# Group 1's head sum by gather and VectorE adds, and the fourth layernorm's statistics on ScalarE, in a two-layer attention and FFN kernel

## The chip, the cores and the metric

One core of one Trainium2 chip runs the whole program. The metric is the device time of one execution in microseconds (us). In the profile lines PE is TensorE (matmuls), PEld its weight loads, DVE VectorE, ACT ScalarE and POOL GpSimd; the granted clock is the share of TensorE's full clock that was granted. Executions of one kernel here agree within 0.2%; all are in the fast state, except three single runs (e4, e6, e7) whose state is unknown. Much of this document measures inside the trace. For that it uses one stretch, called **the stretch** below: from the start of group 0's head-sum matmuls on PE (the first `L<-big,smat` group, near 64 us) to the first matmul of the QKV stage that follows the output projection of group 1 (near 260 us). PE works in a fixed order, so the two ends are the same instructions in every kernel here. The stretch contains everything that the change touches and leaves out the first 64 us, whose length varies from execution to execution with the first loads.

## The reference

Two layers, each a sliding attention (8 keys per position, at distance 0, 2, ..., 14) and a GELU FFN, both with a layernorm without weights and a residual. Cut to what matters:

```python
# x: 1 x 2048 x 1024; H = 32 heads of 32; W = 8 keys, dilation 2; F = 3584
q, k, v = split(layernorm(x) @ wqkv)
logits  = einsum("bhsd,bhswd->bhsw", q, k[pos - 2*w]) * scale     # head sum over d
attn    = softmax(where(pos - 2*w >= 0, logits, -1e9))            # over the 8 keys
x = x + einsum("bhsw,bhswd->bhsd", attn, v[pos - 2*w]) @ wo
x = x + gelu(layernorm(x) @ w1 + b1) @ w2 + b2
# ... the same two lines once more
```

## The kernel before

The 2048 positions are cut into groups of 512; there are eight (layer, group) pairs, numbered n = 0 to 7. PE does all large products (QKV, output projection "wo", FFN1, FFN2) in one fixed order. The attention between them is VectorE work: `new_prod` multiplies q with the shifted k, a tree of adds leaves one product tile, the *head sum* adds the partitions of one head, `attend` is the softmax, `spread` copies its result to all partitions of the head, and `av` makes one of eight weighted sums of v (written to `oT`, which `wo` reads). Groups 0 and 1 did the head sum on PE, the later groups by a DMA gather and three VectorE adds. A drain is VectorE's reading of a finished PSUM bank, `tmp<-acc`, which releases the bank for PE.

```python
bigp = ctx.enter_context(tc.tile_pool(name="bigp", bufs=3))       # 3 big VectorE tiles
def acc_tile():
    return psum.tile([P, T], F32, name="acc", bufs=6)             # 6 PSUM banks for all products
...
def ln_stats_ahead(g):                       # statistics of a layernorm, ahead of its use
    for tt in range(NTT):
        ln_stats(g * NTT + tt, mv_ahead[:, tt, :], rstd_ahead[:, tt, :])   # 2 bn_stats + bn_aggr on VectorE
...
def head_sum(n, last=True):                  # 8 matmuls, four at a time side by side
    ...
    for wh in range(2):
        for tb in range(NTT):
            mm(L[tb * H:(tb + 1) * H, wh * 4:(wh + 1) * 4, :], lhsT=smat[:],
               rhs=prod[:, tb, wh * 4:(wh + 1) * 4, :], ..., tile_position=(0, tb * H))

def gather(n):                               # the other way: move the 4 partitions of a head side by side
    prod = s["prods"].pop(0)
    Lq = bigp.tile([P, HP, W, P], BF16, name="big")
    for j in range(HP):
        pool.dma_start(Lq[:, j, :, :], prod[j::HP, :, :, :])
...
def attend(n):
    e = smp.tile([P, W, P], F32, name="e")
    if "Lq" in s:                            # after gather: three adds
        vec.tensor_tensor(out=e[:], in0=Lq[:, 0, :, :], in1=Lq[:, 1, :, :], op=ALU.add)
        for j in range(2, HP):
            vec.tensor_tensor(out=e[:], in0=e[:], in1=Lq[:, j, :, :], op=ALU.add)
        L = e
    else:
        head_sum(n)
        L = s.pop("L")
    ...
    if n < 2:
        vec.tensor_reduce(out=mx[:], in_=L[:].rearrange("p w t -> p t w"), axis=AX.X, op=ALU.max)
    else:
        mx = fold(L, ALU.max)
    vec.tensor_tensor(out=e[:], in0=L[:], in1=mx..., op=ALU.subtract)
    act.activation(e[:], e[:], ACT.Exp, scale=SCALE)
    ...
def spread(n):
    if n < 2:                                # through DRAM, because the layout is another
        ...
...
# the order of work; (unit, function) pairs hang VectorE work into PE's stages; hold() keeps VectorE's order
stage(gen_ffn1(0), sides=at(5, attend, 1) + at(5, spread, 1) + at(5, hold) + each(new_prod, 2, 2, 1)
      + at(10, gather, 2) + at(10, hold) + each(av, 1, 10, 2, 0, 4))
stage(gen_ffn2(0), sides=at(0, ln_stats_ahead, 3) + at(15, hold) + at(15, ln_a, 3, None, True)
      + each(av, 1, 16, 1, 4, 8) + at(23, hold))
# then gen_wo(1), which reads oT of group 1, and gen_qkv(3)
```

Of the kernel before, what the change touches and what calls it, by code (L numbers as in the profile page):

```python
# [8 lines left out]
ACT = mybir.ActivationFunctionType  # L9
ALU = mybir.AluOpType  # L10
AX = mybir.AxisListType
BF16 = mybir.dt.bfloat16
F32 = mybir.dt.float32
# [4 lines left out]
def kernel(  # L18
# [18 lines left out]
    P = 128  # L37
    _, S, D = A_x.shape
# [3 lines left out]
    W = 8  # L42
# [3 lines left out]
    EPS = 1e-5  # L46
    SCALE = float(DH) ** -0.5
    T = 512
    NTT = T // P
# [4 lines left out]
    HP = P // H  # L54
# [15 lines left out]
    lnp = ctx.enter_context(tc.tile_pool(name="lnp", bufs=2))  # L70
    xnp = ctx.enter_context(tc.tile_pool(name="xnp", bufs=2))
    attp = ctx.enter_context(tc.tile_pool(name="attp", bufs=1))
    bigp = ctx.enter_context(tc.tile_pool(name="bigp", bufs=3))
# [5 lines left out]
    def acc_tile():  # L79
        return psum.tile([P, T], F32, name="acc", bufs=6)  # L80

    class InOrder:
# [18 lines left out]
        def hold(self):  # L101
            self.floor = self.last

    vec, act, pool, sp = InOrder(nc.vector), InOrder(nc.scalar), InOrder(nc.gpsimd), InOrder(nc.sync)
    last_pe = [None]

    def dep_order(dependent, dependency, why):
        tc.add_manual_dep(dependent.ins, dependency.ins.name,
                          mybir.DependencyInfo(mybir.DependencyClass.NoSync, mybir.DependencyReason.SCHED_ONLY), reason=why)
# [7 lines left out]
    def mm(*args, **kwargs):  # L117
        return pe(nc.tensor.matmul(*args, **kwargs))  # L118

    x = [xpool.tile([P, D], BF16, name=f"x{t}") for t in range(S // P)]  # L120
# [26 lines left out]
    mhalf = const.tile([P, 1], F32, name="mhalf")  # L147
# [14 lines left out]
    mv_ahead = const.tile([P, NTT, 2], F32, name="mv_ahead")  # L162
    rstd_ahead = const.tile([P, NTT, 1], F32, name="rstd_ahead")
# [29 lines left out]
    def ln_stats(t, mv=None, rstd=None):  # L193
        stats = lnp.tile([P, 2, 6], F32, name="stats")
        for h in range(2):
            vec.bn_stats(stats[:, h, :], x[t][:, h * HALF:(h + 1) * HALF])
        if mv is None:
            mv = lnp.tile([P, 2], F32, name="mv")
            rstd = lnp.tile([P, 1], F32, name="rstd")
        vec.bn_aggr(mv[:], stats[:])  # L200
        pool.tensor_tensor(out=rstd[:], in0=mv[:, 1:2], in1=eps_t[:], op=ALU.add)
        pool.tensor_tensor(out=rstd[:], in0=rstd[:], in1=mhalf[:], op=ALU.pow)
        return mv, rstd

    def ln_stats_ahead(g):
        for tt in range(NTT):
            ln_stats(g * NTT + tt, mv_ahead[:, tt, :], rstd_ahead[:, tt, :])

    def ln_norm(t, mv, rstd, xn=None):
        if xn is None:  # L210
# [81 lines left out]
    def head_sum(n, last=True):  # L292

        if "L" not in st[n]:
            st[n]["L"] = psum.tile([P, W, P], F32, name="L", bufs=1)
            start = True
        else:
            start = False
        L = st[n]["L"]
        prod = st[n]["prods"].pop(0)  # L300
# [3 lines that stand above are left out]
                   rhs=prod[:, tb, wh * 4:(wh + 1) * 4, :], start=start,  # L304
                   stop=last, skip_group_check=True, tile_position=(0, tb * H))
# [79 lines left out]
    def gather(n):  # L385

        s = st[n]
        prod = s["prods"].pop(0)
        Lq = bigp.tile([P, HP, W, P], BF16, name="big")
        s["Lq"] = Lq  # L390
        for j in range(HP):
            pool.dma_start(Lq[:, j, :, :], prod[j::HP, :, :, :])

    def fold(e, op):

        t = iop.tile([P, W // 2, P], F32, name="tmp")
        vec.tensor_tensor(out=t[:], in0=e[:, 0:4, :], in1=e[:, 4:8, :], op=op)
        vec.tensor_tensor(out=t[:, 0:2, :], in0=t[:, 0:2, :], in1=t[:, 2:4, :], op=op)
        vec.tensor_tensor(out=t[:, 0, :], in0=t[:, 0, :], in1=t[:, 1, :], op=op)
        return t[:, 0, :]  # L400

    def attend(n):

        s = st[n]
        e = smp.tile([P, W, P], F32, name="e")
        if "Lq" in s:
            Lq = s.pop("Lq")
# [7 lines that stand above are left out]
        if n % NG == 0:  # L415
            p = H if n == 0 else P
            vec.tensor_tensor(out=L[0:p, 0:W - 1, 0:HALO], in0=L[0:p, 0:W - 1, 0:HALO], in1=mask[0:p, :, :], op=ALU.add)
        if n < 2:
            mx = smp.tile([P, P], F32, name="mx")
            vec.tensor_reduce(out=mx[:], in_=L[:].rearrange("p w t -> p t w"), axis=AX.X, op=ALU.max)  # L420
            mx = mx[:]
        else:
            mx = fold(L, ALU.max)
        vec.tensor_tensor(out=e[:], in0=L[:], in1=mx.unsqueeze(1).to_broadcast([P, W, P]), op=ALU.subtract)
        act.on = 1 < n < N - 1
        act.activation(e[:], e[:], ACT.Exp, scale=SCALE)
        act.on = False
        z = smp.tile([P, P], F32, name="z")
        vec.reciprocal(z[:], fold(e, ALU.add))
        a = smp.tile([P, W, P], BF16, name="a")  # L430
        vec.tensor_tensor(out=a[:], in0=e[:], in1=z[:].unsqueeze(1).to_broadcast([P, W, P]), op=ALU.mult)
        s["a"] = a

    def spread(n):

        s = st[n]
        a = s.pop("a")
        abc = attp.tile([P, NTT, W, P], BF16, name="abc")
        s["abc"] = abc
        s["oT"] = attp.tile([P, NCH, T], BF16, name="qT" if n == N - 1 else "oT")  # L440
        if n < 2:
            a_d = dram.tile([H, NTT, W, P], BF16, name="a_d")
            for tb in range(NTT):
                pool.dma_start(a_d[:, tb, :, :], a[tb * H:(tb + 1) * H, :, :])
            a = a_d
        for j in range(HP):
            pool.dma_start(abc[j::HP, :, :, :], a[:])
# [33 lines left out]
    def gen_ffn1(n):  # L481
        xnT = xb.pop(n)
        hT = hpool.tile([P, KF, T], BF16, name="hT")
        st[("h", n)] = hT
        for j4 in range(KF // 4):
            wt = wpool.tile([P, KD, 4 * P], BF16, name="wt")
            load = sp.dma_start(wt[:], w1_v[:, :, j4 * 4 * P:(j4 + 1) * 4 * P])
            if n == 0 and j4 == 1:
                dep_order(load, last_transpose[0], "transposes first")
            for jj in range(4):  # L490
                j = j4 * 4 + jj
                ps = acc_tile()
                for k in range(KD):
                    mm(ps[:], lhsT=wt[:, k, jj * P:(jj + 1) * P], rhs=xnT[:, :, k, :], start=(k == 0), stop=(k == KD - 1))
                act.activation(hT[:, j, :], ps[:], ACT.Gelu_apprx_tanh, bias=b1T[:, j:j + 1])
                yield
# [69 lines left out]
    def stage(gen, count=None, sides=()):  # L566


        u = 0
        while count is None or u < count:  # L570
            if next(gen, gen) is gen:
                break
            for v, f in sides:
                if v == u:
                    f()
            u += 1
        for v, f in sides:
            if v >= u:
                f()

    def at(u, f, *args, **kwargs):
        return [(u, lambda: f(*args, **kwargs))]

    def each(f, n, u0, du, c0=0, c1=NCH):
        return [(int(u0 + du * (c - c0)), lambda c=c: f(n, c)) for c in range(c0, c1)]

    hold = vec.hold
# [5 lines left out]
    with tc.tile_pool(name="early", bufs=1) as early:  # L593
        load_x(1)
        load_x(2)
        stage(gen_qkv(0, qk_next=early), sides=at(14, load_b2))
        q1 = gen_qkv(1, defer=True, qk_pool=early)
        stage(q1, sides=at(6, attend, 0) + at(6, spread, 0) + at(6, hold) + each(new_prod, 1, 8, 1, 0, 4) + each(av, 0, 12, 1))
        q2 = gen_qkv(2, defer=True)
        stage(q2, 18)  # L600
        new_prod(1, 4)
        hold()
        stage(gen_wo(0))
        hold()
        stage(q2, sides=each(new_prod, 1, 0, 1, 5, 8))
    hpool = ctx.enter_context(tc.tile_pool(name="hpool", bufs=1))
    stage(gen_ffn1(0), sides=at(5, attend, 1) + at(5, spread, 1) + at(5, hold) + each(new_prod, 2, 2, 1)
          + at(10, gather, 2) + at(10, hold) + each(av, 1, 10, 2, 0, 4))
    stage(gen_ffn2(0), sides=at(0, ln_stats_ahead, 3) + at(15, hold) + at(15, ln_a, 3, None, True) + each(av, 1, 16, 1, 4, 8) + at(23, hold))
    for n in range(1, N - 2):  # L610
# [10 lines left out]
    n = N - 2  # L621
# [35 lines left out]
```

## Time and profile before

| | before |
|---|---|
| time, first three runs | 1233.37 us (1232.91 to 1234.22) |
| PE busy | 1222.2 of 1230.8 us |
| VectorE busy | 861.9 us (70%) |
| the eight matmuls of group 1's head sum | 0.55 us of PE |
| the stretch | 64.19 to 260.56 = 196.37 us |

The busy line of the page: busy us, share of the span, instructions.

```profile
PE 1222.2 (99%) x5739; PEld 632.6 (51%) x5789; DVE 861.9 (70%) x922; ACT 307.3 (25%) x491; POOL 87.2 (7%) x207
```

PE hardly ever waits. The view of waits on PE lists what waited, for what, the sum, how often, and the longest, in us. All three are in the first 15 us:

```profile
PE acc L219 <- DVE xn L93: 1.5, 1, 1.5
PE acc L118 <- DVE big L93: 1.1, 1, 1.1
PE acc L118 <- DMA wt<-in_A_wqkv_dram: 0.3, 1, 0.3
```

PE's timeline (start, length, operation and shapes, count) shows the head sum of group 1 in the middle of FFN1, then FFN2 (`hT`) and wo(1) (`oT`):

```profile
139.05 20.88 PE L118 MATMUL acc<-xnT,wt 128*128 128x512 bf16 x96
159.86 0.62 PE L118 MATMUL L<-big,smat 128*32 128x512 bf16 x8
160.41 38.16 PE L118 MATMUL acc<-xnT,wt 128*128 128x512 bf16 x176
198.40 48.51 PE L118 MATMUL acc<-wt,hT 128*128 128x512 bf16 x219
246.75 13.54 PE L118 MATMUL acc<-wt,oT 128*128 128x512 bf16 x61
```

The head sum takes the time from 159.86 to 160.41, 0.55 us. VectorE is full in this part of the execution. By stretches (window, its length, then busy us and instructions of PE, PEld, DVE, ACT and POOL, the granted clock, DMA share and GB/s), DVE is busy 37.50 of 39 us and 52.94 of 54 us:

```profile
160.00:199.00 39.00, 38.95 (x186) 17.52 (x180) 37.50 (x22) 18.90 (x26) 4.21 (x8) 1.00 0.52 169
199.00:253.00 54.00, 53.74 (x246) 24.46 (x250) 52.94 (x66) 0.29 (x1) 5.55 (x12) 1.00 0.66 205
```

### The profile page before, as it was taken

How to read it: one execution, taken by the hardware profiler on the slowest of the kernel's cores; microseconds unless marked ns; L12 is line 12 of the kernel's file. 1: busy time of each engine (PE TensorE's matmuls, PEld its weight loads, DVE VectorE, ACT ScalarE, POOL GpSimd, SP SyncE). 2: the span in 40 equal slices, each digit the busy share in tenths (PEclk: the TensorE clock that was granted, in tenths of full speed). 3: DMA queues.
4: the chain of work that ended last, by engine and by line, in shares of the span. 5: the costliest groups of instructions: out<-in, count | busy, mean ns of one | idle time of the engine just before them, and what ended most of it. 6: DMA issues, size and time to landing. Idle time of an engine off the chain costs nothing.

```text
span 1230.8 us, 13962 instructions
## 1 busy us (share of the span) xinstructions
PE 1222.2 (99%) x5739; PEld 632.6 (51%) x5789; DVE 861.9 (70%) x922; ACT 307.3 (25%) x491; POOL 87.2 (7%) x207
## 2 busy tenths in 40 slices
PE   9999999999999999999999999999999999999998
PEld 7666544456444564445544465444654444444444
DVE  7989899988998599375993759937599797011001
ACT  4343152014320143202431024310244101400310
POOL 3010010010010000100011000010000002000000
PEclk9999999999999999999999999999999999999999
DMA  9954665656556654856447565486664558446441
GB/s 290 300 179 143 182 222 185 201 154 209 181 165 215 180 162 163 229 172 186 150 163 238 171 171 170 158 223 202 171 196 145 188 196 208 151 158 196 155 135 52
DMA packets 219391, 225.06 MB, mean 183 GB/s; under 512 B 68194, under 2 KB 187136, under 8 KB 217024
## 3 DMA queue, kind: packets, MB, share of 16 engines
q1 hardware_dynamic: 214704, 208.69, 55.5%
q0 software_dynamic: 4624, 15.49, 3.3%
q8 instruction: 45, 0.74, 0.2%
q14 instruction: 18, 0.15, 0.0%
HBM read 191.11 MB, written 4.72 MB: 159 GB/s over the span
## 4 chain that ended last, share of the span: by engine, by line
PE 99%; DMA 1%; issue 0%; SPq 0%; DVE 0%
PE acc L118 98%; DMA wt<-in_A_wqkv_dram 1%; SPq L93 0%; PE L L118 0%; PE L L219 0%; DVE x L93 0%
## 5 line engine op out<-in xcount | busy, mean ns | idle before, releaser
L118 PE MATMUL acc<-xnT,wt 128*128 128x512 bf16 (+1 forms) x3392 | 720.9, 375 | 0.4 <-DMA wt<-in_A_wqkv_dram 0.3
L118 PEld LDWEIGHTS <-wt 128*128 128x128 bf16 x3392 | 400.5, 119 | 319.1 <-issue 1.4
L118 PE MATMUL acc<-wt,hT 128*128 128x512 bf16 (+1 forms) x1780 | 386.0, 376 | 2.1
L118 PEld LDWEIGHTS <-hT 128*128 128x128 bf16 x1820 | 178.1, 98 | 208.9
L93 DVE TENSOR_TENSOR big<-big 128x1024 bf16<-128x1024 bf16 (+2 forms) x184 | 245.2, 1360 | 2.2
L93 ACT ACTIVATE hT<-acc,b1T 128x512 bf16<-128x512 f32 x224 | 152.7, 688 | 332.3 <-PE acc L118 332.1
L93 DVE TENSOR_TENSOR big<-qT,kT 128x4096 bf16<-128x4096 bf16 x64 | 143.8, 2286 | 48.4 <-ACT kT L93 47.8
L93 DVE TENSOR_TENSOR big<-abc,vT 128x4096 bf16<-128x4096 bf16 x64 | 144.7, 2286 | 14.0 <-DMA abc<-a 13.4
L93 DVE TENSOR_TENSOR tmp<-acc,b2bc 128x512 f32<-128x512 f32 x56 | 38.6, 690 | 146.7 <-PE acc L118 143.7
L93 ACT CAST qT<-acc 128x512 bf16<-128x512 f32 (+1 forms) x72 | 38.0, 545 | 351.1 <-PE acc L118 351.1
L118 PE MATMUL acc<-wt,oT 128*128 128x512 bf16 x440 | 97.4, 379 | 0.4
L93 DVE BATCH_NORM_STATS2 stats<-x 128x6 f32<-128x512 bf16 x128 | 85.6, 682 | 4.5 <-DMA x<-in_A_x_dram 3.4
L118 PEld LDWEIGHTS <-oT 128*128 128x128 bf16 x448 | 43.8, 98 | 52.8
L93 DVE TENSOR_TENSOR x<-acc,big 128x512 bf16<-128x512 f32 (+1 forms) x9 | 5.7, 633 | 90.0 <-PE acc L118 90.0
L93 ACT CAST vT<-acc 128x512 bf16<-128x512 f32 x64 | 37.5, 586 | 83.3 <-PE acc L118 83.3
L93 ACT CAST kT<-acc 128x512 bf16<-128x512 f32 x64 | 37.4, 587 | 67.0 <-PE acc L118 67.0
L93 POOL TENSOR_TENSOR rstd<-mv,eps_t 128x1 f32<-128x1 f32 x56 | 14.2, 253 | 515.4 <-DVE mv L93 509.4
L93 DVE TENSOR_TENSOR x<-acc,x 128x512 bf16<-128x512 f32 x64 | 42.9, 671 | 4.8 <-PE acc L118 4.4
L93 DVE TENSOR_SCALAR xn<-x,mv,rstd 128x1024 bf16<-128x1024 bf16 x52 | 28.4, 547 | 20.2 <-POOL rstd L93 20.1
L93 DVE TENSOR_TENSOR x<-tmp,x 128x512 bf16<-128x512 f32 x56 | 38.7, 690 | 1.3
L93 POOL DMA_DIRECT2D big<-big x24 | 13.3, 565 | 256.3 <-DVE big L93 237.6
L93 POOL TENSOR_TENSOR rstd<-rstd,mhalf 128x1 f32<-128x1 f32 x56 | 31.0, 553 | 4.4
(68 smaller groups left out, 228.8 us busy)
## 6 DMA issues: line engine op xcount, KB each, us to landing
wt<-in_B_w_dram SPq DMA_DIRECT2D x56, 1024.0 KB, 5.7
wt<-in_B_w_dram SPq DMA_DIRECT2D x64, 896.0 KB, 4.9
wt<-in_A_wqkv_dram SPq DMA_DIRECT2D x46, 1024.0 KB, 5.6
wt<-in_A_wo_dram SPq DMA_DIRECT2D x16, 1024.0 KB, 5.0
big<-big POOLq DMA_DIRECT2D x24, 256.0 KB, 3.6
abc<-a POOLq DMA_DIRECT2D x24, 256.0 KB, 5.3
x<-in_A_x_dram SPq DMA_DIRECT2D x16, 256.0 KB, 6.2
out_dram<-x SPq DMA_DIRECT2D x31, 128.0 KB, 2.1
```

What stands on the lines that cost most here:

```text
L93: inst = f(*args, **kwargs)
L118: return pe(nc.tensor.matmul(*args, **kwargs))
```

## The change

The intent: group 1 does its head sum as the later groups do, which takes eight matmuls from PE and the trip of the softmax through DRAM; its gather uses a tile (`abc`) that is free at that time. As VectorE is full, the statistics of the fourth layernorm (that of group 3, computed ahead of its use: eight statistics operations and four aggregates) go to ScalarE, which has gaps in the V stage and is idle in FFN2.

```diff
     def ln_stats_ahead(g):
+        junk = lnp.tile([P, D], BF16, name="xn", bufs=3)
         for tt in range(NTT):
-            ln_stats(g * NTT + tt, mv_ahead[:, tt, :], rstd_ahead[:, tt, :])
+            t, mean, var = g * NTT + tt, mv_ahead[:, tt, 0:1], mv_ahead[:, tt, 1:2]
+            less = lnp.tile([P, 1], F32, name="less")
+            act.activation(junk[:], x[t][:], ACT.Identity, scale=-1.0 / D, accum_out=less[:])
+            act.activation(junk[:], x[t][:], ACT.Square, bias=less[:], accum_out=var)
+            pool.tensor_scalar(out=mean, in0=less[:], scalar1=-1.0, scalar2=None, op0=ALU.mult)
+            rstd = rstd_ahead[:, tt, :]
+            pool.tensor_scalar(out=rstd, in0=var, scalar1=1.0 / D, scalar2=EPS, op0=ALU.mult, op1=ALU.add)
+            pool.tensor_tensor(out=rstd, in0=rstd, in1=mhalf[:], op=ALU.pow)
@@ gather
-        Lq = bigp.tile([P, HP, W, P], BF16, name="big")
+        Lq = attp.tile([P, HP, W, P], BF16, name="abc") if n == 1 else bigp.tile([P, HP, W, P], BF16, name="big")
@@ attend (the reduce) and spread (the trip through DRAM)
-        if n < 2:
+        if n == 0:
@@ the order of work
         stage(q2, sides=each(new_prod, 1, 0, 1, 5, 8))
+        gather(1)
-    stage(gen_ffn1(0), sides=at(5, attend, 1) + at(5, spread, 1) + at(5, hold) + each(new_prod, 2, 2, 1)
+    stage(gen_ffn1(0), sides=each(new_prod, 2, 2, 1, 0, 3) + at(5, hold) + at(5, attend, 1) + at(5, spread, 1) + at(5, hold) + each(new_prod, 2, 6, 1, 3, 8)
```

More of the change, by code (lines that the diff above doesn't have):

```diff
@@ L440, in spread @@
         s["oT"] = attp.tile([P, NCH, T], BF16, name="qT" if n == N - 1 else "oT")
-        if n < 2:
+        if n == 0:
             a_d = dram.tile([H, NTT, W, P], BF16, name="a_d")
```

## The prediction

> **What bounds the kernel now.** TensorE. The page has PE busy 1222.2 of 1230.8 us; the chain of work that ended last is 98.4% matmuls into `acc`; the view of waits on PE sums to about 3 us, none on this change's operations. PE steps a 512-column matmul every 219 ns (49 in 10.74 us of the chain). VectorE is over 95% busy in the stretches 160 to 199 and 199 to 253 us, where the change acts, yet PE does not wait for it there.
>
> **What the change does (about 140 to 253 us).**
> - PE loses the eight head-sum matmuls of group 1. The timeline has them from 159.86, and the next ordinary matmul at 160.41: 0.55 us on the chain (384 ns is listed for each, but four run at once; the Trainium skill, "TensorEngine Tiling (Array Packing)", Tiling Modes, gives four tiles at 128x32, and the trace agrees).
> - VectorE loses a max-reduce (1.22), a subtract from PSUM (1.22), eight layernorm statistics (0.68) and four aggregates (0.20): 8.7 us. It gains three 128x1024 adds (3 x 1.22), a max fold (0.69+0.42+0.29) and a subtract (1.22): 6.3 us. Net 2.4 us less, but 3.9 us more before group 1's exponential.
> - ScalarE gains eight 128x1024 passes, by estimate 1.06 us each (the exponential of that size): four between V evacuations (0.59 us of every 1.73), four after the last gelu, where it is idle to 253 us. The instruction order adds no table load.
> - DMA: the softmax's trip through DRAM goes; four SBUF gathers of 256 KB come. POOL gains a few 128x1 operations.
>
> **What is on the critical path.** Only the 0.55 us. Where the additions could reach PE:
> 1. The gather is issued when the product tree ends, 158.8 us. Four issues take 2.2 us and a landing took 3.6 (median): it lands near 164.5. VectorE has 9 us of group 2's products first and reaches the adds near 168. No wait, or tenths at the third product.
> 2. ScalarE now does 12 gelus before the exponential (10 before). VectorE delivers its input near 174.5; with exponential and table load (1.28 us) gelu 13 ends near 177.5. PE needs that bank again at about 180.7: 3 us to spare.
> 3. In the V stage ScalarE falls about 1 us behind; gelus could not start before 154 us anyway, because `hT` waits for the last product.
> 4. At the end of FFN2 VectorE is 2 to 3 us earlier; wo(1) did not wait for it before.
>
> VectorE's relief buys nothing, and the additions cost nothing: PE has no gap to fill.
>
> **Prediction: 1232.8 us** (1233.37 less 0.55), 8 in 10 within 1231.9 to 1234.1. Faster by over 2%: 0.005; within 2%: 0.985; slower by over 2%: 0.01.
>
> **What would show each step.** Chain of waits: one of the two entries of eight head-sum matmuls gone; PE idle unchanged. DVE timeline: adds of `abc` near 168 us without a DMA wait; statistics gone between 200 and 223 us; first FFN2 drain about 3 us earlier, waiting for PE. ACT timeline: passes of about 1.1 us between V evacuations, exponential near 174.5, four passes after the last gelu. DMA: no `a_d` stores for group 1.
>
> **What would make it wrong.** The gather landing later than about 171 us (the DMA engines are full from 149 to 160 us with weights), which would hold the exponential, the gelus and then PE; a ScalarE pass with an accumulator costing far over 1.1 us, or waiting for its scratch buffer in the V stage, so that six banks fill; weight loads delayed by the gather. Each would show as PE waiting for ACT or DMA between 150 and 182 us, and cost 1 to 3 us.

## More of the kernel before

On VectorE's timeline, the statistics lie between the operations of the weighted sums; the last line but one is the last pair of `oT`, the last one the first drain of FFN2's second half (a drain is VectorE's reading of a finished PSUM bank, `tmp<-acc`, which releases the bank for PE):

```profile
199.84 0.69 DVE L93 BATCH_NORM_STATS2 stats<-x 128x6 f32<-128x512 bf16 x1
200.44 2.28 DVE L93 TENSOR_TENSOR big<-abc,vT 128x4096 bf16<-128x4096 bf16 x1
202.63 0.69 DVE L93 BATCH_NORM_STATS2 stats<-x 128x6 f32<-128x512 bf16 x1
...
205.90 2.29 DVE L93 TENSOR_TENSOR big<-abc,vT 128x4096 bf16<-128x4096 bf16 x1 [0.20 <-DMA big<-big]
...
222.19 0.67 DVE L93 TENSOR_TENSOR tmp<-acc,b2bc 128x512 f32<-128x512 f32 x1
...
246.32 0.75 DVE L93 TENSOR_TENSOR oT<-big 128x512 bf16<-128x512 bf16 x2
246.99 0.68 DVE L93 TENSOR_TENSOR tmp<-acc,b2bc 128x512 f32<-128x512 f32 x1
```

So the eighth and last `oT` tile is ready at 246.32 + 0.75 = 247.07 us, the seventh about 0.33 us before it. wo(1) starts at 246.75 and reads the eight tiles in order, one per 219 ns: it comes to the seventh at about 248.06 and to the eighth at about 248.28. That is a margin of about 1.2 us at the eighth (a little more at the seventh).

## The result, and the profile after

The changed kernel took 1232.94 us in the median of six runs (1232.57 to 1233.85), the kernel before 1232.87 (1232.72 to 1234.22). The ratio is 1.000, with a 95% interval of 0.9987 to 1.0013. (Ratios here are the mean time of one kernel's runs over that of the other's runs of the same rounds, so not quite the ratio of the medians that are quoted.) The stretch went from 196.37 to 196.62 us. The 0.55 us of matmuls are gone, and no time was won.

The busy line of the changed kernel: PE has eight instructions fewer.

```profile
PE 1223.3 (99%) x5731; PEld 632.8 (51%) x5781; DVE 861.3 (70%) x915; ACT 315.9 (26%) x507; POOL 94.6 (8%) x211
```

The waits on PE have a line that before did not have, the second:

```profile
PE acc L118 <- DVE big L93: 1.0, 1, 1.0
PE acc L118 <- DVE oT L93: 0.6, 1, 0.6
PE acc L118 <- DMA wt<-in_A_wqkv_dram: 0.5, 1, 0.5
PE acc L227 <- DVE xn L93: 0.2, 1, 0.2
```

PE's timeline shows where. The head sum is gone from FFN1. Six matmuls of wo(1) run, then PE stands for the seventh `oT` tile. From 246.63 to 248.67 are 2.04 us for six matmuls, which need 1.31:

```profile
139.58 58.87 PE L118 MATMUL acc<-xnT,wt 128*128 128x512 bf16 x272
198.29 48.51 PE L118 MATMUL acc<-wt,hT 128*128 128x512 bf16 x219
246.63 1.46 PE L118 MATMUL acc<-wt,oT 128*128 128x512 bf16 x6
248.67 11.52 PE L118 MATMUL acc<-wt,oT 128*128 128x512 bf16 x51 [0.58 <-DVE oT L93]
```

The chain of waits, around 246 us, says the same: it passes from the weighted sums through `oT` to PE, where before it stayed on PE.

```profile
242.60 5.68 DVE big L93 x5
248.28 0.35 DVE oT L93
248.62 0.05 issue
248.67 4.83 PE acc L118 x21
```

VectorE's timeline of the changed kernel has the adds of the gathered tile with no wait ahead of them, then no statistics, but a wait of 1.36 us for the gather of the *next* group:

```profile
168.28 1.22 DVE L93 TENSOR_TENSOR e<-abc 128x1024 f32<-128x1024 bf16 x1
...
204.62 2.29 DVE L93 TENSOR_TENSOR big<-abc,vT 128x4096 bf16<-128x4096 bf16 x1
...
209.39 2.29 DVE L93 TENSOR_TENSOR big<-abc,vT 128x4096 bf16<-128x4096 bf16 x1
213.05 2.29 DVE L93 TENSOR_TENSOR big<-abc,vT 128x4096 bf16<-128x4096 bf16 x1 [1.36 <-DMA big<-big]
215.26 3.55 DVE L93 TENSOR_TENSOR big<-big 128x2048 bf16<-128x2048 bf16 x4
...
224.05 0.68 DVE L93 TENSOR_TENSOR tmp<-acc,b2bc 128x512 f32<-128x512 f32 x1
...
248.20 0.75 DVE L93 TENSOR_TENSOR oT<-big 128x512 bf16<-128x512 bf16 x2
```

By windows, VectorE's 51.54 busy us of 54 are less than before's 52.94, so by busy share it has got lighter; the lines above say that its last result is later.

```profile
160.00:199.00 39.00, 38.95 (x182) 17.70 (x181) 37.36 (x25) 18.82 (x26) 4.12 (x8) 1.00 0.58 194
199.00:253.00 54.00, 53.21 (x244) 24.02 (x247) 51.54 (x53) 4.96 (x9) 12.81 (x16) 1.00 0.67 205
```

ScalarE's timeline: the new passes between V evacuations, each with a second instruction that reads the accumulator out, and the exponential, in its place:

```profile
144.79 1.06 ACT L93 ACTIVATE xn<-x 128x1024 bf16<-128x1024 bf16 x1
145.75 0.19 ACT L93 ACTIVATION_READ_ACCUMULATOR xn<-x 128x1 f32 x1
146.31 1.15 ACT L93 ACTIVATE xn<-x,less 128x1024 bf16<-128x1024 bf16 x1
174.81 1.06 ACT L93 ACTIVATE e<-e 128x1024 f32<-128x1024 f32 x1 [1.96 <-DVE e L93]
```

Counted from the start of the stretch of each trace (the trace's times less 64.19, 64.70, 63.84 and 63.59), VectorE's milestones are these; the last two columns are experiments told below:

| us from the start of the stretch | before | changed | e3: statistics alone | e8: changed, other order |
|---|---|---|---|---|
| VectorE begins group 1's weighted sums (before: their first statistics) | 135.65 | 139.92 | 135.73 | 140.12 |
| first drain of FFN2's first half | 158.00 | 159.35 | 154.06 | 158.10 |
| last `oT` ready | 182.88 | 184.25 | 178.96 | 182.98 |
| PE begins wo(1) | 182.56 | 181.93 | 182.56 | 181.96 |

PE comes to wo(1) 0.63 us earlier and the last `oT` 1.37 us later: 2.0 us, against a margin of about 1.2.

### The profile page after: what moved, and what is told of

Same layout as the page of the kernel before. It is cut to its first block, busy times and chain, and to the rows that moved or that the text cites. A ratio compares the mean times of both kernels' runs of the same rounds, so it can differ in the third digit from the quotient of the medians.

```text
span 1231.5 us, 13960 instructions
## 1 busy us (share of the span) xinstructions
PE 1223.3 (99%) x5731; PEld 632.8 (51%) x5781; DVE 861.3 (70%) x915; ACT 315.9 (26%) x507; POOL 94.6 (8%) x211
## 4 chain that ended last, share of the span: by engine, by line
PE 89%; DVE 8%; DMA 2%; issue 1%; POOL 1%; SPq 0%; ACT 0%; DVEq 0%; POOLq 0%
PE acc L118 89%; DVE big L93 5%; DMA wt<-in_A_wqkv_dram 1%; DMA big<-big 1%; DVE tmp L93 0%; DVE x L93 0%; DVE e L93 0%; DVE stats L93 0%; DMA abc<-big 0%; DVE xn L93 0%; POOL rstd L93 0%; SPq L93 0%; DVE oT L93 0%; POOL abc L93 0%; POOL big L93 0%
## 5 line engine op out<-in xcount | busy, mean ns | idle before, releaser
L93 DVE BATCH_NORM_STATS2 stats<-x 128x6 f32<-128x512 bf16 x120 | 80.1, 680 | 4.9 <-DMA x<-in_A_x_dram 3.9
```

The costliest lines, as they stand in the source:

```text
L93: inst = f(*args, **kwargs)
```

## The experiments

Theory A: the head-sum matmuls were worth their 0.55 to 0.6 us, and the gain was given back at wo(1), because VectorE's last `oT` became late. Theory B, the rival: the matmuls were worth nothing on PE, and VectorE, as predicted, is off the path. All kernels gave the right result but e6. "Before" was timed in the same rounds on the same chip (for the single runs: in the same session), and all compared runs are fast, or single ones (e4, e6, e7) whose trace is read. The stretches, all by the same two instructions:

| run | start, end, stretch us | PE's wait in it (us) | median us (runs) | before, same rounds |
|---|---|---|---|---|
| before | 64.19, 260.56, **196.37** | none | 1232.87 (6) | |
| changed | 64.70, 261.32, **196.62** | oT 0.6 | 1232.94 (6) | 1232.87 |
| e10 changed again | 63.89, 260.64, **196.75** | oT 0.6 | 1232.81 (5) | 1232.69 |
| e1 norms before the drains | 63.54, 263.48, **199.94** | tmp 2.0, weights 0.2 | 1233.70 (5) | 1232.63 |
| e2 gather alone | 64.08, 266.81, **202.73** | tmp 4.2 | 1238.22 (4) | 1232.63 |
| e3 statistics alone | 63.84, 260.21, **196.37** | none | 1232.01 (4) | 1232.63 |
| e4 before, 3.4 us of extra VectorE work | 63.59, 264.52, **200.93** | oT 2.6 | 1236.55 (1) | 1232.63 |
| e5 two norms after the drains | 63.77, 259.54, **195.77** | none | 1231.84 (5) | 1232.62 |
| e6 no head sum (wrong result) | 63.64, 259.42, **195.78** | none | 1231.33 (1) | 1232.62 |
| e7 before, 0.9 us of extra VectorE work | 64.02, 260.84, **196.82** | oT 0.3 | 1232.77 (1) | 1232.62 |
| e8 other order of two weighted sums | 63.59, 259.36, **195.77** | none | 1231.89 (5) | 1232.69 |
| e9 e5 and e8 | 64.69, 260.47, **195.78** | none | 1231.51 (5) | 1232.69 |

### e1: all four normalisations behind the weighted sums

```diff
-    ... at(15, hold) + at(15, ln_a, 3, None, True) + each(av, 1, 16, 1, 4, 8) + at(23, hold))
+    ... at(15, hold) + each(av, 1, 16, 1, 4, 8) + at(19, hold) + at(19, ln_a, 3, None, True) + at(23, hold))
```

> The changed kernel, with the four normalisations of the fourth layernorm moved behind group 1's last weighted sums (about 2 us of VectorE work taken from before the last oT tile). Stretch measured in the trace: from the start of group 0's head sum on PE to the first matmul of the QKV stage after wo(1). Before: 64.19 to 260.56 = 196.37 us; changed kernel: 64.70 to 261.32 = 196.62. Theory A (the head sum's 0.55 us was saved, and given back because the last oT of group 1 came 1.3 us later than before and wo(1) waited): the last oT is ready about 2 us earlier, the wait of PE on oT (0.58) disappears, stretch 195.7 to 195.8 us, that is 0.6 less than before and 0.85 less than the changed kernel. Theory B (the head-sum matmuls were hidden and their removal is worth nothing): wait gone too, but the stretch is 196.4, as before. Whole time: too small for the rounds to show either way, within 0.2% of before.

Neither theory's number came. The wait on `oT` is gone, as both said, but PE waits elsewhere, on the drains of FFN2 (`tmp`), which release its PSUM banks. The waits on PE, then VectorE's timeline:

```profile
PE acc L118 <- DVE tmp L93: 2.0, 1, 2.0
```

```profile
246.27 1.46 DVE L93 TENSOR_SCALAR xn<-x,mv_ahead,rstd_ahead 128x1024 bf16<-128x1024 bf16 x3
250.24 0.55 DVE L93 TENSOR_SCALAR xn<-x,mv_ahead,rstd_ahead 128x1024 bf16<-128x1024 bf16 x1 [2.51 <-DMA xnT<-xn]
250.70 0.69 DVE L93 TENSOR_TENSOR tmp<-acc,b2bc 128x512 f32<-128x512 f32 x1
```

The fourth normalisation needs one of three scratch buffers back from a transposition, waits 2.51 us at the head of VectorE's queue, and all drains stand behind it. The order of the norms and the drains had hidden that. The experiment was badly made and left the question open. It also shows what such a stall can cost. In the windows of this trace, the granted clock (third column from the end) is half for 3.2 us after the wait:

```profile
249.00:251.44 2.44, 0.39 (x3) 0.10 (x2) 1.17 (x3) 0.00 (x0) 0.00 (x0) 1.00 0.99 186
252.20:255.40 3.20, 3.20 (x10) 1.08 (x8) 2.91 (x5) 0.00 (x0) 0.00 (x0) 0.50 0.93 245
```

By their mean clocks only the profiled execution had it (1235.62 us, clock 0.999); the other four, with clock 1.000, took 1233.53 to 1233.91.

### e2: the gather alone

The statistics are put back on VectorE (the change to `ln_stats_ahead` undone).

```diff
     def ln_stats_ahead(g):
-        junk = ...            # and the ScalarE and POOL operations of the change
+        for tt in range(NTT):
+            ln_stats(g * NTT + tt, mv_ahead[:, tt, :], rstd_ahead[:, tt, :])
```

> The changed kernel with the statistics put back on VectorE (the gather alone). Theory A: VectorE carries the gather's adds (4.0 us before the products of group 2 end) and the statistics (about 5 us, of which 1.4 fills the wait for the gather of group 2): it is about 4 us later than before at the last oT, of which PE has 1.1 us in hand; PE stalls 2.5 to 4 us in FFN2 and wo(1) together (waits on DVE tmp and DVE oT), stretch 198.3 to 200.2 us, time about 1235 to 1236. Theory B (VectorE off the path): stretch 196.4 or less.

Measured: 1238.22 us, ratio 1.0045 (1.0031 to 1.0059), stretch 202.73, more than expected. The direction is Theory A's: the gather alone costs, because VectorE's work is on the path. The waits on PE:

```profile
PE acc L118 <- DVE tmp L93: 4.2, 1, 4.2
```

VectorE came to FFN2's first drain so late that PE stood 4.2 us for a bank. The granted clock fell to 0.50 within this wait and stayed there until 234.5 us, 5.25 us of matmuls at half speed, about 2.6 us lost by estimate. Over the 195.77 that the stretch needs without waits (e5, e8), 4.2 and 2.6 make up 6.8 of the 6.96 us. The stall was a little above the upper end of my expectation (4 us), which had no term for the clock.

VectorE's timeline of e2 has a wait for group 2's gather as well, longer than in the changed kernel (1.36 us), although the statistics stand here where they stood in the kernel before:

```profile
212.24 2.29 DVE L93 TENSOR_TENSOR big<-abc,vT 128x4096 bf16<-128x4096 bf16 x1 [2.41 <-DMA big<-big]
```

### e3: the statistics alone

The kernel before, with the changed `ln_stats_ahead` and nothing else.

> The kernel before with only the statistics moved to ScalarE; the head sum of group 1 stays on PE. Both theories: PE keeps its 0.55 us and never waits; stretch 196.3 to 196.4 us, time as before. Theory A further: VectorE is about 2.5 to 3 us earlier than before at the first drain of FFN2 or waits there for PE; and a wait of VectorE of 1 to 2 us for the gather of group 2 shows up near 203 to 207 us, where the statistics had been filling it (0.2 us before).

Measured: stretch 196.37, to the hundredth that of before; 1232.01 us against 1232.63, ratio 0.9996 (0.9981 to 1.0011), unresolved. VectorE is 3.94 us earlier than before at the first drain and waits for PE there, as this line of its timeline shows, so its relief alone moves nothing:

```profile
217.90 0.69 DVE L93 TENSOR_TENSOR tmp<-acc,b2bc 128x512 f32<-128x512 f32 x1 [0.27 <-PE acc L118]
```

One expectation missed: no wait for group 2's gather appears here. e2 and e3 together correct the idea behind it: with the statistics in place and group 1's gather, VectorE waited 2.41 us; without the statistics and without that gather, not at all (0.20 us in before). So the wait comes with group 1's gather, after which group 2's gather takes longer to land (below), and not with the removal of the statistics.

### e4: useless VectorE work in the kernel before

```diff
+    def spend(k):
+        scratch = smp.tile([P, W, P], F32, name="e")
+        vec.memset(scratch[:], 0.0)
+        for _ in range(k):
+            vec.tensor_tensor(out=scratch[:], in0=scratch[:], in1=scratch[:], op=ALU.add)
-    ... at(15, hold) + at(15, ln_a, 3, None, True) + ...
+    ... at(15, hold) + at(15, spend, 2) + at(15, hold) + at(15, ln_a, 3, None, True) + ...
```

> The kernel before with about 3 us of useless VectorE work (a memset and two 128x1024 f32 adds of 1.22 us) put ahead of group 1's last four weighted sums. If wo(1) has only about 1.1 us in hand for oT (read from before: last oT ready 247.0, needed 248.1), PE waits 1.0 to 2.0 us on oT and the stretch grows from 196.37 to between 197.4 and 198.4. If the VectorE work is off the path, as the prediction said of wo(1), the stretch stays 196.4.

Measured: stretch 200.93, 4.56 us more; that VectorE is off the path is refuted for the kernel before. The size was missed, again upwards. The last `oT` came 4.10 us later than in before (250.57 - 63.59 against 182.88), more than the added work, in part because the fourth normalisation waited 0.36 us for a transposition. PE waited for `oT` 2.6 us, and then ran at a granted clock of 0.50 for some 3.4 us, by estimate 1.7 us lost.

```profile
PE acc L118 <- DVE oT L93: 2.6, 2, 2.0
```

### e5: two normalisations behind FFN2's last drains

```diff
-    ... at(15, ln_a, 3, None, True) + each(av, 1, 16, 1, 4, 8) + at(23, hold))
+    ... at(15, ln_a, 3, None, True, 0, 2) + each(av, 1, 16, 1, 4, 8) + at(23, hold)
+        + at(31, hold) + at(31, ln_a, 3, None, True, 2, 4) + at(31, hold))
```

(`ln_a` takes the first and the last tile as two more arguments.)

> The changed kernel, with the last two of the fourth layernorm's four normalisations moved behind FFN2's last drains, so that neither the last oT nor the drains wait for them (e1 had moved all four ahead of the drains, where the fourth had to wait 2.5 us for one of three scratch buffers, and PE then waited for a bank). Theory A: last oT about 1 us earlier than in the changed kernel, PE waits on oT at most 0.1 us, no wait on drains, clock 1.000 throughout: stretch 195.7 to 195.9 us (before 196.37, changed kernel 196.62). Theory B (removing the head sum is worth nothing): 196.3 to 196.5. A transposition that lands after the next stage's start would show as PE waiting on a transpose instead, and would leave the question open. The whole time: 0.5 us less than before, less than the rounds resolve.

Measured: 195.77 us, Theory A's number. PE's waits have no `oT` and no `tmp`; the granted clock is 1.000. The time is 1231.84 us (1231.48 to 1232.14) against 1232.62 (1232.27 to 1233.63): ratio 0.9993 (0.9980 to 1.0007), so the rounds alone do not show a gain, though every run of e5 is below every run of before.

### e6: the head sum left out (wrong result)

e3's kernel, in `attend`:

```diff
+        elif n == 1:
+            vec.tensor_copy(e[:], s["prods"].pop(0)[:, 0, :, :])
+            L = e
         else:
             head_sum(n)
```

> Wrong result on purpose: the kernel of e3 (statistics on ScalarE) with group 1's head-sum matmuls left out and one copy of 128x1024 in their place. VectorE keeps about 3 us in hand, so nothing can take the saving back. Theory A: stretch 195.75 us, 0.6 less than e3's 196.37. Theory B: 196.3 to 196.4.

Measured: 195.78 us, 0.59 less than e3. This is the price of the eight matmuls by themselves, and Theory B is refuted.

### e7: a small dose

```diff
-    at(15, spend, 2)
+    at(15, spend, 0)
```

> e4's kernel with the memset alone (0.91 us in e4's trace), a dose at about the 1.1 us that wo(1) has in hand. Theory A: PE waits on oT at most 0.4 us, stretch 196.3 to 196.8, clock 1.000; against 200.93 for e4's dose of 3.4 us: a threshold, not a proportion.

Measured: 196.82, two hundredths over the range. The last `oT` came 1.56 us later than in before (more than the memset, in part because the fourth normalisation waited 0.29 us) and the stretch grew 0.45, so 1.1 us were absorbed. The changed kernel gives the same margin: 2.0 us later against PE, 0.85 us lost (196.62 - 195.77), 1.15 absorbed.

### e8: another order of two weighted sums

One `hold`: the second weighted sum is finished before the third's product begins. VectorE does the same operations.

```diff
-    ... + at(10, gather, 2) + at(10, hold) + each(av, 1, 10, 2, 0, 4))
+    ... + at(10, gather, 2) + at(10, hold) + each(av, 1, 10, 2, 0, 4) + at(12, hold))
```

> The changed kernel, with one change of order on VectorE: the second weighted sum of group 1 is finished before the product of the third is begun. In the changed kernel the third's product stood ahead of the second's adds and waited 1.36 us for the gather of group 2 to release its buffer, and the adds, which were ready, queued behind it. Theory A: that wait is gone (0.1 us or less), the first drain of FFN2 and the last oT come about 1.1 us earlier against the start, PE no longer waits for oT, stretch 195.7 to 195.9 us, as in e5, though not an operation was taken from VectorE. If the lateness came from the amount of VectorE work and not from this wait, the stretch stays near 196.6.

Measured: stretch 195.77, no wait of PE. VectorE's timeline, to be held against the lines of the changed kernel from 204.62 on:

```profile
208.48 2.29 DVE L93 TENSOR_TENSOR big<-abc,vT 128x4096 bf16<-128x4096 bf16 x1
210.81 1.95 DVE L93 TENSOR_TENSOR big<-big 128x2048 bf16<-128x2048 bf16 x2
212.79 0.42 DVE L93 TENSOR_TENSOR oT<-big 128x512 bf16<-128x512 bf16 x1
213.14 4.48 DVE L93 TENSOR_TENSOR big<-abc,vT 128x4096 bf16<-128x4096 bf16 x2
```

The adds fill the time in which the buffer is not yet free, and nothing waits. The first drain and the last `oT` come 1.25 and 1.27 us earlier than in the changed kernel. The time is 1231.89 us (1231.30 to 1232.16) against 1232.69 (1232.19 to 1233.41): ratio 0.9992 (0.9979 to 1.0006).

### e9 and e10: both repairs; the changed kernel once more

> e5 and e8 together: VectorE has about 2 us more in hand. PE has no more gap to give back: stretch 195.7 to 195.85 us, no better than e5 or e8 alone. Time about 1231.8 to 1232.1, against 1232.6 of before, an interval that may still hold 1.

> The changed kernel as it is, beside e8 and e9 on the same chip. Stretch 196.6 again, wait on oT 0.4 to 0.7 us. Time 0.5 to 1 us above e8 and e9, if the execution's start is alike.

e9 measured 195.78 us: VectorE has still more in hand, and PE gains nothing by it. Its time was 1231.51 us (1231.48 to 1232.44), ratio 0.9991 (0.9979 to 1.0004). e10 repeated the changed kernel: 196.75 us, 1.42 us of VectorE waiting for the gather, 0.64 us of PE waiting for `oT`, and 1232.81 us (1232.18 to 1233.87) beside 1231.89 of e8 and 1231.51 of e9 on the same chip. So the versions that are to be preferred over both kernels are e5, e8 and e9: 0.6 us less than before in the stretch. Their whole times (0.8, 0.8 and 1.2 us below before) agree with that in sign, but their intervals do not exclude no change.

## Why the prediction was right or wrong

The time fell in the range: 1232.94 us measured against 1232.8 predicted. But the mechanism was only half right, and the number agreed because the gain, and what took it back, are each smaller than the scatter of runs. It was luck in one more way: 1232.8 was reckoned from the first three runs of before (1233.37); from the median of all six (1232.87) the same reckoning gives 1232.3.

- **"0.55 us on the chain": right.** The column-tiled matmuls cost 0.55 us by the timeline and 0.59 to 0.60 by e6, e5 and e8. What the Trainium skill, "TensorEngine Tiling (Array Packing)", Tiling Modes, says of four tiles at 128x32 agrees with it: 8 matmuls in 0.55 us, where eight of 219 ns one after the other would be 1.75.
- **The gather lands in time (step 1): right.** The adds began at 168.28 with no wait. **ScalarE before the exponential (step 2): right**, the exponential started at 174.81, and PE did not wait. **The V stage (step 3): right.** The passes took 1.06 and 1.15 us instead of 1.06, plus 0.19 for reading the accumulator. The Trainium skill, "ScalarE: Activation LUTs", What ACT_TABLE_LOAD costs, gives 186 ns + 0.833 ns per element, and 93 ns more with a pointer operand: by estimate from these figures 1.04 and 1.13 us for 1024 elements, in agreement.
- **"At the end of FFN2 VectorE is 2 to 3 us earlier": wrong.** It was 1.37 us later. The 3.9 us before the exponential came as predicted (4.27 us at the start of the weighted sums, all in all). The saving of the statistics was the term that was mis-sized. From the start of the weighted sums to the first drain, VectorE took 22.35 us before and 19.43 after: 2.9 us saved where I had counted 6.2 (8 x 0.68 + 4 x 0.20). Three things are in the gap. Read from start to start, the statistics occupied only 5.0 us, because the listed durations of neighbours overlap by about 0.09 us each (a statistics operation of 0.69 us is followed by the next start after 0.60 us, an aggregate of 0.20 us after 0.12). Without them the operations of one weighted sum follow each other in dependent order and overlap less; 0.9 us is left for this. And VectorE waited 1.36 us for the gather of group 2, against 0.20 before. e8 shows that the last of these, with the order that let it hold up ready work, is enough: with the same operations in another order PE's wait and all but 0.1 us of the lateness are gone.
- **"wo(1) did not wait for it before", and so "the additions cost nothing": wrong as an argument.** The absence of a wait was read as freedom, and the margin was not measured. It was about 1.2 us (read from before; e7 and the changed kernel absorbed 1.1 and 1.15), and removing 0.6 us of PE work ahead of it makes it smaller by as much. With VectorE 1.37 us later, PE lost 0.85 us, more than the 0.60 gained: 196.37 - 0.60 + 0.85 = 196.62. The timeline gives the loss without this sum: 0.73 us ahead of the seventh matmul (2.04 less 1.31), and about 0.1 more because the eighth tile is ready 0.33 us after the seventh, where PE steps 0.22.
- **The risks named:** none of the three came. The gather that mattered was the next one, of group 2. In the changed kernel it was issued 4.7 us later within FFN2 (205.16 - 198.29 against 200.53 - 198.40), and its four pieces landed 5.7 to 6.2 us after their issue (the same gather in before: 3.4 to 3.6, in e3 3.5 to 3.9). The DMA engines were busy 0.82 to 1.06 from 206 to 214 us. They were as busy in before while its gather ran (0.70 to 1.08 from 200 to 206 us), so why this one took longer is left open. One candidate is in the traces: an FFN2 weight transfer issued at 204.5 us, just before the gather, landed after 5.7 us, where the one issued at 198.6 in before, 1.9 us ahead of its gather, landed after 4.7; e2 and e8 have the same 5.7 and gathers of up to 5.9 and 6.0. No run tested it. In e8 the gather was as slow as in the changed kernel, so what e8 mended was the order alone.

Shown by experiment: that the matmuls are worth 0.6 us, that the loss is at wo(1), that at the late gather of group 2 the order of VectorE's queue makes the lateness (e8), and that the statistics' move is needed (without it, e2, 5.6 us are lost). Argued only: the split of the missing 3.3 us (6.2 less 2.9) among overlap and dependent order. Open: why the gather landed later.

## What to carry to other kernels

When PE is 99% busy, an engine beside it that causes no wait may still be one microsecond from causing one. Before moving work, read for each hand-over to PE the margin, the time from the producer's end to the consumer's start, and take off it both what the producer loses and what PE gains. An in-order queue also makes the order of operations worth time by itself: in the changed kernel a product that was blocked by a late gather stood ahead of adds that were ready, and e8 won the time back without removing an operation. And look at what follows a removed operation, not at its listed duration alone: of the 6.2 us of statistics, removing them saved 2.9 us here, and 4.4 us where nothing waited (22.35 less 17.98 in e8).

## What the Trainium skill lacked or had wrong

- "TensorE: Matmul & The Clock Gate", Part 1 and Why this matters for your kernels: the array is said to fall to half its clock after an idle window of about 3.4 us, and the rule given is no idle gap of over about 3 us. In e1 one wait of 2.05 us was followed by a granted clock of 0.50 for about 3.4 us, in one of five executions; in e4 two waits, 1.96 and 0.67 us, had the same effect. The changed kernel's 0.58 us and e7's 0.28 us had none. The length of the slow phase in e1 and e4 does agree with the page's window of about 3.4 us; in e2, with a wait of 4.20 us, it was about twice that (from about 227.7 to 234.5 us).
- "ScalarE: Activation LUTs", What it computes: an accumulator output is mentioned without its cost. Here it is a second instruction of 0.19 us after each pass.
